# Softmax attention with a gated MLP on one Trainium2 core: next x loaded a block sooner, gate weights behind it, strips kept in order, the exponential table asked for in block one, projected sums put into rows of x

## The chip, the cores and the metric

The kernel runs on one core of one Trainium2 chip. The metric is the device time of one execution in microseconds (us); before the change the median of three runs is 2617.08 us (2616.3 to 2622.25).

## What is computed

All tensors are float32. S is 2048 rows, D is 576, F is 4608; there are 32 heads of 18 features.

```python
xn = layernorm(x)                                   # [S, D]
q, k, v = split(xn @ wqkv)                          # 32 heads x 18
o = softmax(q @ k.T * 18 ** -0.5) @ v               # per head, [S, S] scores
s = o @ wo
gate, up = xn @ W_gate, xn @ W_up                   # [S, F]
g = silu((gate * (gate > 0) * up) @ W_down)
out = x + s * g
```

Products are taken in float32 precision by splitting each operand into a rounded high part and a low remainder and adding three matmuls (high by high, high by low, low by high).

## The kernel before

**Stages.** The first 200 us normalize x, transpose it in nine chunks of 64 features per group of 512 rows, split it in high and low parts, project q, k and v, and write x, q, k and v back to HBM as `xTd`, `qd`, `kd`, `vd`. The rest is a line of 144 *blocks* `k`, made by `emit_unit` (L897). Block k works on group g of 512 rows (4 groups) and on f, one of 36 slices of 128 MLP features, so g changes at k = 36, 72 and 108; in these notes "boundary 1" is the step from block 35 to block 36, and so on. A block's first half (`up`, L696) multiplies nine chunks of x by gate and up weights (tiles `pg`, 54 matmuls on two halves of the array at once). Attention is woven into it: score matmuls for row maxima (`pm`, from `max_steps`, L244) of head pair u + 1 and score matmuls for the exponentials (`psx`, from `exp_steps`, L855) of head pair u. Sixteen blocks come before the first pair; then each of the 16 pairs u takes eight blocks. An odd block ends with 64 matmuls of attention times v (`po`, `attend`), an even one with 48 of the down projection (`py`, `down`). So two blocks are `pg`…, `po`, `pg`…, `py`.

**x.** `load_x` (L297) brings a chunk of x back from `xTd` in two DMAs (512 KB together) into pool `xA`, which has eleven buffers for the nine chunks of a group. In the last block of a group, `up` asks for the first two chunks of the next group ahead of its matmuls, and for chunk c + 2 after the last matmul that reads chunk c (L707, L717).

**Weights.** `load_up(k)` (L283) brings gate and up weights of block k (two DMAs, 576 KB together, tile `rg`, one buffer; `p` for blocks 3 to 15), `split_up` (L292) splits them on GpSimd (tile `gw`), a block ahead. `emit_unit` asks for block k + 2 at its start. `load_down` and `split_down` do the same for the down weights (`rd`, `dw`, 288 KB).

**Strips.** `strips` (L217) fetches q or k of one head pair in six small DMAs into a ring: `load_q` (tiles `kq`, `qT`) and `load_k` (`kA`, `kq`).

**Order.** Matmuls and most VectorE and GpSimd work are kept in program order. DMAs are issued by SyncE (queue SP). Its class `Maybe` keeps program order while `sp.kept` is true; from block 10 on it is false, and a scheduler may put an SP DMA anywhere its operands allow, also far ahead of where the program asks for it; `load_x` alone is always pinned. A DMA that waits on SP holds up all behind it.

**The end.** In the last head pair's block 6 four row tiles of the output are projected (`project`, L985: s in PSUM times the gate tile `gt`, then plus the row tile `xt`, then stored) with two sets of buffers; `rows_of` (L1005) loads the gate rows from `gd` and the rows of x for tile j + 2 into the buffers of tile j. In the profile these tiles are all called `gx`.

Of the kernel before, what the change touches and what calls it, by code (L numbers as in the profile page):

```python
# [9 lines left out]
F32 = mybir.dt.float32  # L10
F32R = mybir.dt.float32r
AF = mybir.ActivationFunctionType
# [7 lines left out]
def kernel(  # L20
# [11 lines left out]
    P = 128  # L32
# [77 lines left out]
    ident = consts.tile([P, P], F32, name="ident")  # L110
    make_identity(nc, ident)
    mark = consts.tile([P, 1], F32, name="mark")
    qd = dram.tile([2, D, S], F32, name="qd")
    kd = dram.tile([2, D, S], F32, name="kd")
    vd = dram.tile([NU, P, NT, HW], F32, name="vd")
# [11 lines left out]
        nc.scalar.activation(dhi, ps, AF.Copy)  # L127
        nc.vector.tensor_tensor(dlo, ps, dhi.bitcast(F32), ALU.subtract)

    def split_pool(hi, lo, raw):  # L130
        gp.tensor_copy(hi, raw)
        gp.tensor_tensor(lo, raw, hi.bitcast(F32), ALU.subtract)

    PRODUCTS = ((0, 0), (0, 1), (1, 0))

# [79 lines left out]
    tasks = []  # L215

    def strips(dst, src, u, cs, order):  # L217
        for h in range(2):
            f0 = (2 * u + h) * DH
            for b, i in enumerate(order):  # L220
                r0 = h * R + b * DH
                sp.dma_start(dst[r0 : r0 + DH].bitcast(F32), src[i, f0 : f0 + DH, cs])

    def kchunk(u, c):
        return ring[(NQ * u + c) % NRING]
# [82 lines left out]
    with ExitStack() as st:  # L308
# [2 lines left out]
        xB = pool(xBs, "xB", XC, "right")  # L311
        hx = pool(xBs, "hx", 4, "right")

        def weights(name, n, parts, pl=one, held=None, **kw):

            sl = WS if len(parts[0]) == 2 else XC
            gw = homes_w[name] if name in homes_w else pl.tile([P, 2, WS, n], F32R, name=name, **kw)
            gw = gw[:, :, :sl]
            o = 0
            for cols in parts:  # L320
                m = sum(c[2] for c in cols[0])
                rg = one.tile([P, WS, P], F32, name="rgw", bufs=2)[:, :sl, :m]
                load_nat(rg, cols)
                hi, lo = gw[:, 0, :, o : o + m], gw[:, 1, :, o : o + m]

                if held is not None:
                    held += [hi, lo, rg]
                else:
                    split_pool(hi, lo, rg)
                o += m  # L330
            return gw

# [233 lines left out]
        def qk_weights(b, **kw):  # L566
            wqk.append(
                weights(f"wqk{b}", P, [[[(wqkv, b * P, P)], [(wqkv, D + b * P, P)]]], **kw)
            )
# [4 lines left out]
        for _ in range(57):  # L574
            tp(warm[:, :P], ident, ident)
        first_rows(rows0, *held)
        qk_weights(1)
        nxt = load_rows(1)
        wvs = []

# [18 lines left out]
        for g in range(NQ):  # L599
# [46 lines left out]
            if last:  # L646
                mx = [max_steps(0, h) for h in range(2)]
                both = zip(*mx)
                deal[:] = [both, (P1 + P2) // 3, 0]
                homes = [  # L650
                    lambda: [bank("pv") for _ in range(2)],
                    lambda: [shared("pv") for _ in range(2)],
                    lambda: [psO.tile([P, 512], F32, tag="po", name="pv"), shared("pv")],
                    lambda: [bank("pv") for _ in range(2)],
                ]
                for j in range(4):
                    v_job(wv, g, j, homes[j]())
                    if j == 0:
                        split_up(1)
                    if j == 2:  # L660
                        load_up(2)
                deal[0] = None
                flush()
                for c in range(KC + 2 - XC, KC):
                    load_x(0, c)
            else:
                for j in range(4):
                    v_job(wv, g, j)
                    if j == 0 and g == 0:
                        nxt = load_rows(g + 2)  # L670
                    if j == 1:
                        spill(g, marks[-1] if g == 0 else None)
                    if j and g == NQ - 2:
                        for c in range(2 * j - 2, 2 * j):
                            load_x(0, c)
                if fill is not None:
                    for _ in fill:
                        pass
# [17 lines left out]
    def up(k):  # L696

        g, f = units[k]
        gw = gus.pop(k)
        if k < N1 and (k % 2 == 0 or k == N1 - 1):  # L700
            ps = [psO.tile([P, 512], F32, name="po"), shared("pg2")]
        else:
            ps = [bank("pg0"), bank("pg1")]
        last = f == NF - 1 and k + 1 < len(units)
        if last:
            for c in range(2):
                load_x(units[k + 1][0], c)  # L707
        xg = xcur[g]

        def ops(t, c, i, j, rows):  # L710
            return gw[rows, i, c, :], xg[c][rows, j, :]

        def half(t):
            for n, _ in enumerate(row_half(ps[t], ops, t)):
                c = n // len(PRODUCTS)
                if t and last and n % len(PRODUCTS) == 2 and c + 2 < KC:
                    load_x(units[k + 1][0], c + 2)  # L717
                yield

        return ps, [half(t) for t in range(2)]  # L720
# [72 lines left out]
    def run_tasks(todo):  # L793
        while todo:
            fn, args = todo.pop(0)
            fn(*args)
# [100 lines left out]
    def emit_unit(k, ex, ns, mx, nm):  # L897
# [5 lines left out]
        if k not in rds and k not in dws:  # L903
            load_down(k)
        split_up(k + 1)
        if k:
            load_up(k + 2)
        if k == 10:
            sp.kept = False
# [26 lines left out]
        if k == 0:  # L936
            split_up(2)
        up_end(k, ps)
        run_tasks(tasks)
        if k % 2:  # L940
            run_tasks(outs)
# [40 lines left out]
        vec(nc.vector.tensor_tensor(o5[DT:P], raw5[DT:P], o5[DT:P].bitcast(F32), ALU.subtract))  # L982
        return hf, o5

    def project(k, hf, o5, gt, xt, last=False):  # L985

        for m in range(2):
            cs = slice(m * HC, (m + 1) * HC)
            ps = shared("pw")[:, :HC]
            prs = []  # L990
            for c in range(4):
                w = wos[c]
                prs += [(hf[:, 0, c], w[:, 0, cs]), (hf[:, 0, c], w[:, 1, cs]), (hf[:, 1, c], w[:, 0, cs])]
            prs += [(o5, wos[4][:, i, cs]) for i in range(2)]
            for i, (l, w) in enumerate(prs):
                mm(ps, l, w, start=(i == 0), stop=(i == len(prs) - 1))
            vec(nc.vector.tensor_tensor(gt[:, cs], ps, gt[:, cs], ALU.mult))  # L997
            if last:
                vec(nc.vector.tensor_tensor(gt[:, cs], gt[:, cs], xt[:, cs], ALU.add))
                sp.dma_start(out2[k * P : (k + 1) * P, cs], gt[:, cs])  # L1000
        if not last:
            gp.tensor_tensor(gt, gt, xt, ALU.add)
            sp.dma_start(out2[k * P : (k + 1) * P, :], gt)

    def rows_of(k, gt, xt):  # L1005
        if k not in kept:
            sp.dma_start(gt, gd[k * P : (k + 1) * P, :])
        sp.dma_start(xt, x2[k * P : (k + 1) * P, :])

    inputs = {}  # L1010

# [15 lines left out]
    for u in range(NU):  # L1027
# [8 lines left out]
        for i in range(PER):  # L1036
# [3 lines left out]
            if not more:  # L1040
# [10 lines left out]
                if i == 6:  # L1051
# [6 lines left out]
                    split_down(k)  # L1058
                    load_down(k + 1)
                    for j in range(4):  # L1060
                        project(j, *inputs.pop(j))
                        rows_of(j + 2, sy[j % 2], sx[j % 2])
                        inputs[j + 2] = *split_heads(j + 2, spare[j % 2]), sy[j % 2], sx[j % 2]
                        if j < 2:
                            load_heads(j + 4)
                        if j == 1:
                            split_down(k + 1)
            k += 1
# [47 lines left out]
```

## Time and profile before

The profiled execution took 2619.22 us; its span, from first to last instruction, is 2617.5 us.

| | us | what it is |
|---|---|---|
| median of three runs | 2617.08 | the metric |
| profiled execution | 2619.22 | one run, its own time |
| its span | 2617.5 | the scale of all times below |
| PE busy | 2595.6 | TensorE matmuls, 99% of the span |
| DVE, ACT, POOL busy | 1907.2, 1385.3, 1204.6 | VectorE, ScalarE, GpSimd |
| PE waiting for x from HBM | 11.5 | 14 waits of at most 1.7 |

PE is the matmul engine, PEld its weight load. A row of the timeline gives start, length, engine, line, operation, out<-in by tile names, and in brackets the idle time before it and what ended it. A PE row's length is modelled, so a matmul that was held up can look busy: where time is lost is better read from how far the starts of successive pieces lie apart.

### The profile page before, as it was taken

Reading aid. Unit: us, or ns where it says so; the run is one execution under the profiler, and the core shown is the slowest. Engines: PE = TensorE matmul, PEld = TensorE weight load, DVE = VectorE, ACT = ScalarE, POOL = GpSimd, SP = SyncE. Lnnn points to the kernel's source line nnn. Section 1 sums busy time; section 2 is a strip of 40 time slices with the busy share of each in tenths; the row PEclk is TensorE's granted clock in tenths of the full one; section 3 lists DMA queues with packets and bytes.
Section 4 is the critical chain, followed back from the end, with each engine's and each line's share of the span. In section 5 each row is a group of like instructions: output and inputs, shape, how many; then the busy total and the mean of one; then the engine's idle time right before and its main releaser. Section 6 shows DMA issues by size and latency. Waiting matters only on the chain.

```text
span 2617.5 us, 54137 instructions
## 1 busy us (share of the span) xinstructions
PE 2595.6 (99%) x21845; PEld 2039.3 (78%) x21845; DVE 1907.2 (73%) x3141; ACT 1385.3 (53%) x2594; POOL 1204.6 (46%) x971
## 2 busy tenths in 40 slices
PE   9999999999999999999999999999999999999999
PEld 8898887877677777777767777787767777777788
DVE  5336677888778888888877888888877888888145
ACT  3221136655565556655556555666556655556552
POOL 4246764444364444444444444444435444444554
PEclk9999999999999999999999999999999999999999
DMA  8866422223542223222363322332254232222345
GB/s 253 274 210 159 101 55 74 66 65 75 126 104 67 71 68 80 60 72 63 76 148 85 71 71 67 75 71 71 65 126 104 70 74 66 72 58 58 71 136 190
DMA packets 263802, 253.08 MB, mean 97 GB/s; under 512 B 27648, under 2 KB 208896, under 8 KB 263552
## 3 DMA queue, kind: packets, MB, share of 16 engines
q1 hardware_dynamic: 255808, 222.48, 34.3%
q0 software_dynamic: 7744, 27.14, 3.0%
q8 instruction: 172, 2.82, 0.5%
q14 instruction: 78, 0.64, 0.1%
HBM read 203.01 MB, written 46.01 MB: 95 GB/s over the span
## 4 chain that ended last, share of the span: by engine, by line
PE 93%; DMA 3%; POOL 1%; DVE 1%; issue 1%; SPq 1%; ACT 0%; POOLq 0%; ACTq 0%; DVEq 0%
PE pg L68 31%; PE py L68 18%; PE po L68 17%; PE pm L68 11%; PE psx L68 9%; PE pq L68 3%; DMA x<-xTd 2%; PE pv L68 2%; PE pw L68 2%; POOL gw L85 0%; POOL dw L85 0%; SPq L301 0%; PE tps L76 0%; SPq L97 0%; DMA qd<-hh 0%
## 5 line engine op out<-in xcount | busy, mean ns | idle before, releaser
L270 DVE TENSOR_REDUCE mx<-pm 128x1 f32<-128x512 f32 x2048 | 1364.8, 690 | 374.0 <-PE pm L68 215.7
L68 PE MATMUL pg<-x,gw 64*128 64x512 f32 x7533 | 1376.2, 394 | 11.5 <-DMA x<-xTd 11.5
L97 ACT ACTIVATE p<-psx 128x512 f32<-128x512 f32 x2048 | 1099.6, 603 | 494.1 <-PE psx L68 444.5
L68 PEld LDWEIGHTS pg<-x,gw 64*128 64x128 f32 x7533 | 1028.9, 187 | 109.1 <-DMA x<-xTd 18.6
L85 POOL TENSOR_TENSOR hh<-h,hh 128x512 fp32r<-128x512 f32 x144 | 185.4, 1288 | 1014.3 <-ACT hh L97 970.7
L68 PEld LDWEIGHTS py<-dw,hh 128*128 128x128 f32 x3456 | 461.2, 189 | 25.9 <-DVE mx L270 18.0
L68 PE MATMUL py<-dw,hh 128*128 128x288 f32 x3456 | 478.0, 297 | 0.0
L68 PE MATMUL po<-p,va 128*32 128x512 f32 x4096 | 452.7, 594 | 0.0
L85 POOL TENSOR_TENSOR gw<-rg,gw 128x1152 fp32r<-128x1152 f32 x131 | 350.1, 2672 | 10.5
L68 PEld LDWEIGHTS po<-p,va 128*32 128x32 f32 x4096 | 126.6, 110 | 291.4 <-issue 280.7
L757 DVE TENSOR_TENSOR y<-py,y 128x288 f32<-128x288 f32 x544 | 237.0, 453 | 113.5 <-PE py L68 113.3
L68 PE MATMUL psx<-qT,kq 56*128 56x512 f32 x608 | 230.7, 393 | 0.0
L68 PE MATMUL pm<-kq,qT 54*128 54x512 f32 x608 | 228.5, 399 | 0.4 <-DVE mx L270 0.4
L85 POOL TENSOR_TENSOR dw<-rd,dw 128x576 fp32r<-128x576 f32 x144 | 206.4, 1433 | 11.5
L97 ACT ACTIVATE hh<-h 128x512 fp32r<-128x512 f32 x144 | 90.9, 631 | 214.1 <-DVE h L728 214.1
L68 PE MATMUL psx<-kq,kA 56*128 56x512 f32 x512 | 196.0, 394 | 0.2 <-DVE h L728 0.2
L68 PE MATMUL pm<-kq 54*128 54x512 f32 x512 | 195.4, 402 | 0.0
L68 PE MATMUL pm<-kA,kq 54*128 54x512 f32 x512 | 193.8, 399 | 0.9 <-DVE mx L270 0.9
L68 PE MATMUL psx<-kq 56*128 56x512 f32 x512 | 194.6, 392 | 0.0
L85 POOL CAST dw<-rd 128x576 fp32r<-128x576 f32 x144 | 95.9, 666 | 167.7 <-PE py L68 157.0
L68 PE MATMUL pm<-kA,qT 54*128 54x512 f32 x416 | 160.2, 403 | 0.0
L68 PE MATMUL psx<-qT,kA 56*128 56x512 f32 x416 | 158.4, 395 | 1.4 <-DVE gx L997 1.4
(96 smaller groups left out, 2274.1 us busy)
## 6 DMA issues: line engine op xcount, KB each, us to landing
rd<-in_B_W_down_dram SPq DMA_DIRECT2D x144, 288.0 KB
rg<-in_B_W_gate_dram SPq DMA_DIRECT2D x131, 288.0 KB
rg<-in_B_W_up_dram SPq DMA_DIRECT2D x131, 288.0 KB
x<-xTd SPq DMA_DIRECT2D x72, 256.0 KB
qd<-hh POOLq DMA_DIRECT2D x16, 512.0 KB, 4.2
kd<-hh POOLq DMA_DIRECT2D x16, 512.0 KB, 5.6
xTd<-x SPq DMA_DIRECT2D x16, 512.0 KB
kq<-kd SPq DMA_DIRECT2D x210, 36.0 KB
```

The source lines that it names most:

```text
L68: return tc.keep_in_program_order(nc.tensor.matmul(*args, **kw))
L85: return lambda *args, **kw: tc.keep_in_program_order(op(*args, **kw))
L97: i = op(*args, **kw)
L270: vec(nc.vector.tensor_reduce(mx[:, h, b, j, c : c + 1], ps, axis=AX.X, op=ALU.max))
L757: vec(nc.vector.tensor_tensor(ys[j][:, cs], ps, ys[j][:, cs], ALU.add))
```

## The change

Five edits, none of which alters a number that is computed.

1. **x and gate weights.** The first two chunks of the next group are asked for at the start of the last block but one (f = 34, `units[k + 2]`). In the last block `load_up(k + 2)` moves from the block's start to behind the request for chunk 4. Before block 0, `load_up(2)` moves behind the requests for x.
2. **Strips** of head pairs 0, 1 and 2 are pinned in program order.
3. **Exponential table.** A one-column Exp at the end of block 0.
4. **First weights.** The low part of the second q/k weight tile is made in four pieces instead of one, in the order 2, 2, 3, 2 of its nine slots.
5. **End.** The sum goes into the rows of x; the gate rows of tile j + 2 are asked for right after the sum, ahead of the store, and the rows of x after the next heads.

```diff
-    def split_pool(hi, lo, raw):
+    def split_pool(hi, lo, raw, pieces=(slice(None),)):
         gp.tensor_copy(hi, raw)
-        gp.tensor_tensor(lo, raw, hi.bitcast(F32), ALU.subtract)
+        for s_ in pieces:
+            gp.tensor_tensor(lo[:, s_], raw[:, s_], hi[:, s_].bitcast(F32), ALU.subtract)
...
     def strips(dst, src, u, cs, order):
+        queue = Kept(nc.sync) if u < 3 else sp
...
-                sp.dma_start(dst[r0 : r0 + DH].bitcast(F32), src[i, f0 : f0 + DH, cs])
+                queue.dma_start(dst[r0 : r0 + DH].bitcast(F32), src[i, f0 : f0 + DH, cs])
...
-        qk_weights(1)
+        qk_weights(1, pieces=(slice(0, 2), slice(XC, XC + 2), slice(2, XC), slice(XC + 2, WS)))
...
-                    if j == 2:
-                        load_up(2)
                 deal[0] = None
                 flush()
                 for c in range(KC + 2 - XC, KC):
                     load_x(0, c)
+                load_up(2)
...
         last = f == NF - 1 and k + 1 < len(units)
-        if last:
+        if f == NF - 2 and k + 2 < len(units):
             for c in range(2):
-                load_x(units[k + 1][0], c)
+                load_x(units[k + 2][0], c)
...
                     load_x(units[k + 1][0], c + 2)
+                    if c == 2:
+                        load_up(k + 2)
...
-        if k:
+        if k and (units[k][1] < NF - 1 or k + 1 == len(units)):
             load_up(k + 2)
...
         up_end(k, ps)
+        if k == 0:
+            pinned(nc.scalar.activation(first_exp, ident[:, :1], AF.Exp))
...
-            gp.tensor_tensor(gt, gt, xt, ALU.add)
-            sp.dma_start(out2[k * P : (k + 1) * P, :], gt)
+            gp.tensor_tensor(xt, gt, xt, ALU.add)
+            if refill:
+                refill()
+            sp.dma_start(out2[k * P : (k + 1) * P, :], xt)
...
-                        project(j, *inputs.pop(j))
-                        rows_of(j + 2, sy[j % 2], sx[j % 2])
+                        project(j, *inputs.pop(j), refill=lambda: gate_of(j + 2, sy[j % 2]))
                         inputs[j + 2] = *split_heads(j + 2, spare[j % 2]), sy[j % 2], sx[j % 2]
                         if j < 2:
                             load_heads(j + 4)
+                        x_of(j + 2, sx[j % 2])
```

`gate_of` and `x_of` are the two halves of `rows_of`. The order of instructions on PE and DVE is the same as before; ACT's has the table load moved and one activation more, POOL's three pieces more; SP's changes most. The rows below are SP's queue.

SP around boundary 1, before: x<-xTd are the loads of x (18 DMAs, nine chunks), rd the down weights of blocks 35 and 36, rg the gate and up weights of blocks 37 and 38, od<-on attention results stored in block 34.

```order
L97 DMA od<-on 18x512 x2
L97 DMA rd<-in_B_W_down_dram 128x576
L97 DMA rg<-in_B_W_gate_dram 64x9x128
L97 DMA rg<-in_B_W_up_dram 64x9x128
L301 DMA x<-xTd 64x1024 x18
L97 DMA rd<-in_B_W_down_dram 128x576
```

The same place now:

```order
L97 DMA od<-on 18x512 x2
L304 DMA x<-xTd 64x1024 x4
L97 DMA rd<-in_B_W_down_dram 128x576
L304 DMA x<-xTd 64x1024 x6
L97 DMA rg<-in_B_W_gate_dram 64x9x128
L97 DMA rg<-in_B_W_up_dram 64x9x128
L304 DMA x<-xTd 64x1024 x8
L97 DMA rd<-in_B_W_down_dram 128x576
```

Two chunks moved past the down weights into block 34, three more past the gate weights of block 37, and those stand ahead of the last four. Boundaries 2 and 3 read alike.

SP ahead of block 0, before: qT<-qd are q strips of head pair 1, kA<-kd k strips of pair 2, rg the weights of block 2, rd those of block 0.

```order
L97 DMA kq<-kd 18x512 x6
L97 DMA qT<-qd 18x1024 x12
L97 DMA rg<-in_B_W_gate_dram 64x9x128
L97 DMA rg<-in_B_W_up_dram 64x9x128
L97 DMA kA<-kd 18x512 x6
L301 DMA x<-xTd 64x1024 x6
L97 DMA rd<-in_B_W_down_dram 128x576
```

The same place now:

```order
L85 DMA kq<-kd 18x512 x6
L304 DMA x<-xTd 64x1024 x6
L97 DMA rg<-in_B_W_gate_dram 64x9x128
L97 DMA rg<-in_B_W_up_dram 64x9x128
L97 DMA rd<-in_B_W_down_dram 128x576
```

Eighteen strips left this place for that of the program's request (around blocks 13 to 16), and x stands ahead of the weights of block 2.

SP in the projections, before: gx<-gd are gate rows, gx<-in_A_x_dram rows of x, out_dram<-gx stores, ro and r heads.

```order
L97 DMA out_dram<-gx 128x576
L97 DMA gx<-in_A_x_dram 128x576
L97 DMA ro<-od 128x4x128
L97 DMA r_32981<-od 64x128
L97 DMA gx<-gd 128x576
L97 DMA out_dram<-gx 128x576
```

The same place now:

```order
L97 DMA gx<-gd 128x576
L97 DMA out_dram<-gx 128x576
L97 DMA ro<-od 128x4x128
L97 DMA r_32986<-od 64x128 x2
L97 DMA gx<-in_A_x_dram 128x576
L97 DMA gx<-gd 128x576
```

The gate rows moved ahead of the store, the rows of x behind the heads.

More of the change, by code (lines that the diff above doesn't have):

```diff
@@ L112 @@
     mark = consts.tile([P, 1], F32, name="mark")
+    first_exp = consts.tile([P, 1], F32, name="first_exp")
     qd = dram.tile([2, D, S], F32, name="qd")
@@ L312, with weights @@
         hx = pool(xBs, "hx", 4, "right")
-        def weights(name, n, parts, pl=one, held=None, **kw):
+        def weights(name, n, parts, pl=one, held=None, pieces=(slice(None),), **kw):
             sl = WS if len(parts[0]) == 2 else XC
@@ L328, in weights @@
                 else:
-                    split_pool(hi, lo, rg)
+                    split_pool(hi, lo, rg, pieces)
                 o += m
@@ L983, in split_heads, with project @@
         return hf, o5
-    def project(k, hf, o5, gt, xt, last=False):
+    def project(k, hf, o5, gt, xt, last=False, refill=None):
         for m in range(2):
@@ L1001, in project, with gate_of, x_of, rows_of @@
         if not last:
-            gp.tensor_tensor(gt, gt, xt, ALU.add)
-            sp.dma_start(out2[k * P : (k + 1) * P, :], gt)
-    def rows_of(k, gt, xt):
+            gp.tensor_tensor(xt, gt, xt, ALU.add)
+            if refill:
+                refill()
+            sp.dma_start(out2[k * P : (k + 1) * P, :], xt)
+    def gate_of(k, gt):
         if k not in kept:
             sp.dma_start(gt, gd[k * P : (k + 1) * P, :])
+    def x_of(k, xt):
         sp.dma_start(xt, x2[k * P : (k + 1) * P, :])
+    def rows_of(k, gt, xt):
+        gate_of(k, gt)
+        x_of(k, xt)
     inputs = {}
```

## The prediction

> **What bounds the kernel now.** I read the page first: the busy time by engine and the shares of the chain that ended last.
>
> ```profile
> PE 2595.6 (99%) x21845; PEld 2039.3 (78%) x21845; DVE 1907.2 (73%) x3141; ACT 1385.3 (53%) x2594; POOL 1204.6 (46%) x971
> ...
> PE 93%; DMA 3%; POOL 1%; DVE 1%; issue 1%; SPq 1%; ACT 0%; POOLq 0%; ACTq 0%; DVEq 0%
> ```
>
> TensorE sets the time. No edit removes a matmul, so the only thing to gain is time in which PE is held up, and 99% busy says little about it, since a matmul that is held up counts as busy. So I went to the chain in order of time, where every block pair shows its `po` piece, and looked for pairs that are too long.
>
> ```profile
> 626.29 7.00 PE po L68 x64
> ...
> 660.31 7.00 PE po L68 x64
> 677.54 6.16 PE py L68 x45
> ...
> 736.44 7.00 PE po L68 x64
> ...
> 1281.65 7.00 PE po L68 x64
> ...
> 1354.89 7.00 PE po L68 x64
> ...
> 1899.86 7.00 PE po L68 x64
> ...
> 1974.74 7.00 PE po L68 x64
> ```
>
> A pair of blocks takes 660.31 - 626.29 = 34.02 us. The two pairs that hold boundary 1 take 736.44 - 660.31 = 76.13 where 68.04 is due: **8.1 us lost**. Boundary 2: 1354.89 - 1281.65 = 73.24, **5.2 lost**. Boundary 3: 1974.74 - 1899.86 = 74.88, **6.8 lost**. Together 20.1 us, three places in 2617. What happens there is in the table of 4 us windows (stretch, its length, busy time of PE, PEld, DVE, ACT and POOL, granted clock, DMA share, GB/s) and, for boundary 1, in the timelines of SP and of PE.
>
> ```profile
> 700.00:704.00 4.00, 4.00 (x36) 2.50 (x30) 2.18 (x4) 2.50 (x5) 3.35 (x5) 1.00 1.03 255
> ...
> 712.00:716.00 4.00, 2.41 (x14) 1.44 (x16) 1.48 (x3) 1.69 (x3) 0.00 (x0) 0.81 1.14 234
> 716.00:720.00 4.00, 4.00 (x18) 3.16 (x15) 2.85 (x5) 1.03 (x2) 0.00 (x0) 0.50 0.16 31
> ```
>
> ```profile
> 669.79 0.90 SPq L97 DMA_DIRECT2D od<-on  x2
> 685.96 0.36 SPq L97 DMA_DIRECT2D rd<-in_B_W_down_dram  x1
> 689.83 0.60 SPq L97 DMA_DIRECT2D rg<-in_B_W_gate_dram  x1
> ...
> 692.02 14.99 SPq L301 DMA_DIRECT2D x<-xTd  x18
> ```
>
> ```profile
> 713.57 0.50 PE L68 MATMUL pg<-x,gw 64*128 64x512 f32 x1 [1.68 <-DMA x<-xTd]
> ```
>
> The first load of x is issued at 692.02, behind gate weights that wait for their buffer until 689.83, though block 35 began at about 684.1 (the `py` piece at 677.54 plus 6.5). From then the DMA engines are full (share 1.03, 255 GB/s), and PE waits for chunk after chunk until 713.57. Then the granted clock falls to 0.50 for some 4 us.
>
> **Boundaries.** The move takes the wait's cause away. Nine chunks came in 713.57 - 692.02 = 21.55 us, 2.4 us each. Now two of them are asked for behind the od stores (669.79, block 34), sixteen us before the rush. At 685.96, behind the down weights, chunk 2 follows as soon as PE has left chunk 0; then 3, 4, the gate weights, 5 to 8. By sizes in the code the down and gate weights are 0.55 and 1.1 chunks, so 7 + 0.55 + 1.1 = 8.65 chunks at 2.4 us end at 686.4 + 20.8 = 707.2. PE begins block 36 at about 701.3 and reads nine chunks in a block's 10.2 us (677.54 - 667.3, the `po` end at 660.31 + 7.0), so it needs chunk 8 at 701.3 + 9.0 = 710.3, and chunk 5, which lands near 700, at 707. Margin 3 us or more for each. So the waits should go entirely: **20.1 us**, bounds 15 (what a residue of a little under 2 us a boundary leaves) and 20.1. What is late next: the gate weights of block 37, issued at about 690 as now but landing some 6 us later, near 697; GpSimd splits them from 701, so that is hidden by half of block 35. The chunks moved into block 34 pass nothing that PE waits for there.
>
> The fallen clock is part of those 20.1 us: boundary 2 lost 5.2 with the clock at full rate, boundaries 1 and 3 lost 2.9 and 1.6 more.
>
> ```profile
> 1332.00:1336.00 4.00, 2.64 (x18) 1.58 (x18) 2.04 (x4) 2.17 (x4) 0.00 (x0) 1.00 1.07 251
> ...
> 1952.00:1956.00 4.00, 2.46 (x14) 1.77 (x14) 1.29 (x3) 1.19 (x2) 0.00 (x0) 0.69 1.10 213
> ```
>
> I take it to go with the waits, since it comes right behind the longest of them. The Trainium skill (TensorE: Matmul & The Clock Gate, section "What's actually happening") says that the array falls to half rate after at least one idle window of about 3.4 us; here it fell after waits of at most 1.68 us each, so either the windows count something softer than idleness or the fall is not the waits' own. By the rule read strictly the 4.5 us stay (a rival below).
>
> **Block 0.** The same in small, by the timelines of SP and PE.
>
> ```profile
> 195.75 5.47 SPq L301 DMA_DIRECT2D x<-xTd  x6
> ```
>
> ```profile
> 204.91 0.39 PE L68 MATMUL po<-x,gw 64*128 64x512 f32 x1
> ...
> 205.13 0.39 PE L68 MATMUL po<-x,gw 64*128 64x512 f32 x1
> ...
> 207.07 0.50 PE L68 MATMUL pg<-x,gw 64*128 64x512 f32 x1 [1.49 <-DMA x<-xTd]
> ```
>
> Starts lie 0.22 us apart, then 1.94: 1.7 us lost. The loads wait for buffers that PE leaves only at about 195, so they cannot start much sooner; but the strips and weights in front of them are gone. I take half, **0.9 us**, bounds 0 and 1.8. The weights of block 2, now behind x, land near 207, when GpSimd comes to split them; if they are late, block 2 waits for at most the 1 to 2 us they moved.
>
> **Strips.** Of the strips that the scheduler had pulled forward, twelve ran just when stores of q were due (SP, ACT, PE timelines):
>
> ```profile
> 179.00 7.59 SPq L97 DMA_DIRECT2D qT<-qd  x12
> ```
>
> ```profile
> 184.80 0.60 ACT L127 ACTIVATE hh<-pq 128x512 fp32r<-128x512 f32 x1 [1.49 <-DMA qd<-hh]
> ```
>
> ```profile
> 186.77 0.50 PE L68 MATMUL pm<-kA,kq 54*128 54x512 f32 x1 [0.95 <-DVE mx L270]
> ```
>
> ACT waits 1.49 us for a store to leave its buffer, VectorE stands behind it, PE 0.95 us behind that. Without the strips: **0.9 us**, bounds 0 and 1.2. At their new places, between blocks 13 and 24, they are hidden by blocks of 17 us; if not, six of them cost the 3.8 us that half of the row at 179.00 shows.
>
> **Table.** The load of the exponential's table, ACT's idle time behind block 0, and PE's starts around the load:
>
> ```profile
> 360.32 1.28 ACT L97 ACT_TABLE_LOAD   x1
> ```
>
> ```profile
> 215.03 0.60 ACT L97 ACTIVATE h<-pg 128x512 f32<-128x512 f32 x1 [4.77 <-PE pg L68]
> ```
>
> ```profile
> 360.42 0.50 PE L68 MATMUL psx<-kq,kA 56*128 56x512 f32 x1
> 361.08 0.50 PE L68 MATMUL psx<-kq,kA 56*128 56x512 f32 x1 [0.16 <-DVE h L728]
> ...
> 362.02 0.49 PE L68 MATMUL pm<-kq,qT 54*128 54x512 f32 x1 [0.44 <-DVE mx L270]
> ```
>
> Gaps of 0.66 and 0.94 where 0.22 is usual: **1.2 us**, nearly the load's length. Behind block 0 ACT is idle for 4.77 us, so the load costs nothing there; bounds 0.9 and 1.3. The Trainium skill (ScalarE: Activation LUTs, "What ACT_TABLE_LOAD costs") puts a switch at 2.66 us with a drain, which would make this term 2.6 and the sum 1.4 larger; the row shows 1.28.
>
> **First weights.** GpSimd's low part (POOL) and PE behind it:
>
> ```profile
> 15.28 2.67 POOL L85 TENSOR_TENSOR wqk<-rgw,wqk 128x1152 fp32r<-128x1152 f32 x1
> ```
>
> ```profile
> 18.01 16.26 PE L68 MATMUL pq<-x,wqk 64*128 64x512 f32 x140 [0.50 <-POOL wqk L85]
> ```
>
> The first two pieces, 4/9 of 2.67 us, end at about 16.6, before PE comes at 17.5: **0.8 us** with the slowed matmul ahead of the gap, bounds 0.3 and 1.0. Three more starts on GpSimd cost it about 0.2 us, where nobody waits.
>
> **End.** The chain and PE's row:
>
> ```profile
> 2538.36 1.81 POOL gx L85
> 2540.17 0.02 issue
> 2540.19 3.19 DMA out_dram<-gx
> ...
> 2543.43 4.59 DMA gx<-gd
> ```
>
> ```profile
> 2548.65 0.86 PE L68 MATMUL psx<-qT,kA 56*128 56x512 f32 x2 [1.36 <-DVE gx L997]
> ```
>
> PE waits for a PSUM bank that VectorE empties only when gate rows have come, and these wait for a store to leave their buffer. Now they start at the sum's end, 2540.2, and come 3.2 us sooner, which is more than PE's wait: **1.6 us** with the slowed restart, bounds 0 and 1.8. Late next are the rows of x of tiles 2 and 3, behind heads and, for tile 3, behind gate rows of tile 4 on SP. GpSimd's sums wait for them, and behind those on GpSimd the remainder `hh` of the last block; PE has that block's `pg` and 7 us of `po` to cover it.
>
> **Sum.** 20.1 + 0.9 + 0.9 + 1.2 + 0.8 + 1.6 = 25.5 us. PE runs without a break between these places and to the last projection, so I let all of it reach the end. The profiled execution took 2619.22 us by its own time: 2593.7. It lies 2.1 over the median of the runs, 2617.08, so the median should come to **2591.6 us**. All lower bounds give 15 + 0 + 0 + 0.9 + 0.3 + 0 = 16.2, so 2600.9; all upper ones 27.2, so 2589.9.
>
> **Rivals.**
>
> *The clock falls all the same.* If the half-rate stretch at boundaries 1 and 3 comes from the clock's own windows and not from the waits, 4.5 us stay: 2596.1. For it: it follows waits of 1.7 us only, and boundary 2, with waits in all of its last chunks, has none. Against: it comes right behind the longest waits. Chance 0.08. (This is what the strict reading of the page on the clock gate, cited above, gives.)
>
> *x is still late.* If the DMA engines, with stores and strips beside them, bring a chunk only every 3.0 us, chunk 8 lands at 686.4 + 26 = 712.4, 2 us after its need; at 3.6 us a chunk it is 7 us. Of the gain 6 to 15 us would go, and the time would be 2598 to 2607. For it: the share is already over 1 there, and GpSimd's stores use the same engines. Against: the 2.4 us were measured under just that load. Chance 0.08 for more than 2600.
>
> *The wait moves to the gate weights.* PE is through with x, but the weights of block 37, now behind three chunks, reach GpSimd late, and block 37 waits in place of block 36. Block 37 starts at 718 if nothing waits (701.3 + 10.2 + 6.5), and a split takes GpSimd about 4 us, so to eat 6 us a boundary they would have to land near 720, over 20 us later than I reckon. Then the gain is some 7 us: 2610, no change that can be told. Chance 0.04.
>
> *Slower: strips block the queue.* In program order a strip waits on SP until PE has left its ring buffer, and the down and gate weights behind it wait too. Eight groups of strips (of pairs 1 and 2) are concerned. Weights are asked for two blocks ahead and split one ahead, so a wait under one block (17.0 us, half of 34.02) costs nothing, and what exceeds it costs PE in full. If each group stood 21 us, 8 x 4 = 32 us are lost: 2591.6 + 32 = 2623.6. Against: the order on SP puts each group next to weights of the block in which its buffer comes free. Chance 0.03.
>
> That the change does not do what it says I rule out: the order on SP shows x ahead, and PE's and VectorE's orders are unaltered.
>
> **The numbers.** The forecast has 0.77, the fallen clock 0.08, late x 0.08, weights 0.04, strips 0.03. The range 2588 to 2600 holds the first two (0.85, a little less for their tails): its ends are the sums of the bounds, with a microsecond or two for the runs' scatter below. A difference of 0.3%, 7.9 us, is about what a measurement of this kernel can tell from no change. Faster by more needs under 2609.2: forecast, clock and late x, 0.93. Within: 0.04. Slower: 0.03.
>
> **What would show it.** In the new profile the `po` pieces around each boundary lie 68 us apart, no PE row around block 36 has a wait for x, and the granted clock stays at 1.00 there; the table load stands near 209; PE's gaps near 185, 206, 360 and 2547 are gone. I am wrong if PE waits for x or for `gw` in blocks 36 to 38, or if a pair of blocks between 16 and 40 takes more than 34.1 us.

## The result and the profile after

| | before | after |
|---|---|---|
| median of 6 runs (lowest, highest) | 2618.61 us (2616.30, 2622.25) | 2601.21 us (2600.33, 2602.55) |
| profiled execution, its own time | 2619.22 us | 2600.33 us |
| its span | 2617.5 us | 2598.6 us |

The ratio is 0.9933, with a 95% interval of 0.992 to 0.9946: faster, by 17.4 us. The forecast was 2591.6 us, range 2588 to 2600. So the direction came, and a third of the gain did not.

The page of the kernel after, busy time by engine and the chain's shares by engine:

```profile
PE 2589.2 (100%) x21845; PEld 2017.2 (78%) x21845; DVE 1912.9 (74%) x3141; ACT 1382.1 (53%) x2595; POOL 1204.4 (46%) x974
...
PE 98%; DVE 1%; DMA 1%; POOL 0%; issue 0%; SPq 0%; ACT 0%; POOLq 0%; ACTq 0%
```

DMA's share of the chain fell from 3% to 1%. The chain in order of time shows the boundaries, each row a `po` piece (start, length):

```profile
662.01 7.00 PE po L68 x64
...
696.03 7.00 PE po L68 x64
...
730.30 7.00 PE po L68 x64
...
1275.38 7.00 PE po L68 x64
...
1343.70 7.00 PE po L68 x64
...
1888.87 7.00 PE po L68 x64
...
1957.17 7.00 PE po L68 x64
```

The two pairs at a boundary now take 68.29, 68.32 and 68.30 us, where 76.13, 73.24 and 74.88 stood. TensorE's order is the same in both kernels, so the start of one and the same matmul can be held against itself. At boundary 1 the `po` piece goes from 1.70 us late (662.01 against 660.31) to 6.14 early (730.30 against 736.44): 7.84 us won. Boundary 2: 6.27 to 11.19 early, 4.92 won. Boundary 3: 10.99 to 17.57, 6.58. Together 19.3 of the 20.1 forecast. No wait of PE for x or `gw` is left between 684 and 724 us, and the 4 us windows that had a clock of 0.81, 0.50 and 0.69 are at full rate (columns as before: PE, PEld, DVE, ACT, POOL, clock, DMA share, GB/s):

```profile
712.00:716.00 4.00, 4.00 (x33) 3.55 (x30) 3.96 (x9) 1.90 (x4) 0.00 (x0) 1.00 0.17 46
716.00:720.00 4.00, 4.00 (x31) 3.84 (x31) 2.40 (x7) 0.00 (x0) 1.80 (x2) 1.00 0.49 139
...
1952.00:1956.00 4.00, 4.00 (x37) 3.37 (x36) 3.29 (x7) 3.85 (x8) 3.83 (x5) 1.00 0.53 123
```

But look at the first of those `po` rows: at 662 us the changed kernel is 1.7 us **behind**, where the terms of the opening (0.8, 0.9, 0.9, 1.2) should have put it 3.8 ahead. 5.5 us are missing, all of them ahead of 370 us. Held against itself at many places, the same matmul tells where:

| stretch (us) | what happens | forecast | won (+) or lost (-) |
|---|---|---|---|
| to 18 | first weights | +0.8 | +0.7 |
| 20 to 35, 104 to 132 | `pq` matmuls run slower | 0 | -0.8 |
| 184 to 189 | strips | +0.9 | +0.8 |
| 203 to 209 | x of block 0 | +0.9 | +0.6 |
| 217 to 224 | block 2 waits | 0 | -2.4 |
| 228 to 359 | blocks 2 to 15 run slower | 0 | -1.0 |
| 359 to 370 | table | +1.2 | +0.5 |
| 684 to 1960 | boundaries | +20.1 | +19.3 |
| 2530 to 2612 | end | +1.6 | +1.4 |

The nine rows add to 19.1 us; the span lost 18.9. Three of the rows were forecast at nothing. One is **block 2**. The timelines of SP and of POOL, kernel after:

```profile
195.08 5.77 SPq L304 DMA_DIRECT2D x<-xTd  x6
200.95 0.63 SPq L97 DMA_DIRECT2D rg<-in_B_W_gate_dram  x1
201.62 0.90 SPq L97 DMA_DIRECT2D rg<-in_B_W_up_dram  x1
```

```profile
210.07 1.15 POOL L85 CAST gw<-rg 128x1152 fp32r<-128x1152 f32 x1 [6.40 <-DMA rg<-in_B_W_up_dram]
211.31 2.67 POOL L85 TENSOR_TENSOR gw<-rg,gw 128x1152 fp32r<-128x1152 f32 x1
213.93 1.29 POOL L85 TENSOR_TENSOR hh<-h,hh 128x512 fp32r<-128x512 f32 x1
...
220.42 0.66 POOL L85 CAST dw<-rd 128x576 fp32r<-128x576 f32 x1 [3.06 <-DMA rd<-in_B_W_down_dram]
```

The same two casts in the kernel before:

```profile
208.11 1.15 POOL L85 CAST gw<-rg 128x1152 fp32r<-128x1152 f32 x1 [3.77 <-PE po L68]
...
218.46 0.67 POOL L85 CAST dw<-rd 128x576 fp32r<-128x576 f32 x1 [3.08 <-DMA rd<-in_B_W_down_dram]
```

Before, GpSimd came to the weights when PE had left their buffer; now it stands 6.40 us for their transfer, which the chain shows as one piece of 8.31 us from its issue:

```profile
201.62 8.31 DMA rg<-in_B_W_up_dram
```

What stood in its way is not x alone: GpSimd issued four stores of v (288 KB each) at 193.45 and 199.82, and from 194 to 211 us the engines moved 3.65 MB. GpSimd's work is kept in program order, so the remainder `hh`, the down weights and the request for the next ones (`rd`, in the buffer that GpSimd has to empty) all move by 2 us, and the `py` of block 2 waits twice on PE's timeline:

```profile
222.62 0.40 PE L68 MATMUL py<-dw,hh 128*128 128x288 f32 x1 [0.96 <-POOL dw L85]
223.85 2.40 PE L68 MATMUL py<-dw,hh 128*128 128x288 f32 x16 [0.82 <-POOL hh L85]
```

The other two are a **slower TensorE**, with no wait at all. The timeline of PE has a run of a hundred `pq` matmuls near 110 us, before and after:

```profile
109.95 11.55 PE L68 MATMUL pq<-x,wqk 64*128 64x512 f32 x100
```

```profile
109.58 11.84 PE L68 MATMUL pq<-x,wqk 64*128 64x512 f32 x100
```

And in the chain, from one `py` to the fourth behind it (eight blocks), before 82.63 us (263.33 to 345.96), after 83.25:

```profile
263.33 6.55 PE py L68 x48
...
345.96 6.55 PE py L68 x48
```

```profile
264.93 6.59 PE py L68 x48
...
348.18 6.59 PE py L68 x48
```

The granted clock is 1.00 in all of it. Behind 370 us nothing more is lost to it: from 378 to 660 us the changed kernel takes 281.7 us and the kernel before 281.8. So the theories: (a) block 2's weights behind x cost 2.4 us; (b) something slows TensorE in these stretches, and the candidates are the strips at their new places, the table loaded early, the way PE restarts after a wait, and, after the first four experiments, the places of the tiles in memory.

### The profile page after: what moved, and what is told of

It reads as the page before. It is cut to its first block, busy times and chain, and to the rows that moved or that the text cites. A ratio compares the mean times of both kernels' runs of the same rounds, so it can differ in the third digit from the quotient of the medians.

```text
span 2598.6 us, 54145 instructions
## 1 busy us (share of the span) xinstructions
PE 2589.2 (100%) x21845; PEld 2017.2 (78%) x21845; DVE 1912.9 (74%) x3141; ACT 1382.1 (53%) x2595; POOL 1204.4 (46%) x974
## 4 chain that ended last, share of the span: by engine, by line
PE 98%; DVE 1%; DMA 1%; POOL 0%; issue 0%; SPq 0%; ACT 0%; POOLq 0%; ACTq 0%
PE pg L68 31%; PE po L68 19%; PE py L68 18%; PE pm L68 11%; PE psx L68 10%; PE pq L68 4%; PE pw L68 2%; PE pv L68 2%; PE tps L76 0%; DMA rg<-in_B_W_up_dram 0%; DMA xt<-in_A_x_dram 0%; POOL dw L85 0%; DMA rd<-in_B_W_down_dram 0%; POOL hh L85 0%; DVE hh L129 0%
## 5 line engine op out<-in xcount | busy, mean ns | idle before, releaser
L68 PE MATMUL pg<-x,gw 64*128 64x512 f32 x7533 | 1362.2, 393 | 0.9 <-DMA x<-xTd 0.9
L68 PEld LDWEIGHTS pg<-x,gw 64*128 64x128 f32 x7533 | 1016.9, 186 | 97.2 <-issue 4.0
L85 POOL CAST gw<-rg 128x1152 fp32r<-128x1152 f32 x131 | 157.3, 1201 | 12.1 <-DMA rg<-in_B_W_up_dram 12.1
```

The lines of the kernel that those rows point to most:

```text
L68: return tc.keep_in_program_order(nc.tensor.matmul(*args, **kw))
L85: return lambda *args, **kw: tc.keep_in_program_order(op(*args, **kw))
```

## The experiments

All times below are medians of 4 to 11 runs, beside medians of the kernel before of 2619.0 to 2619.9 us on the same chips; the profile of each gives the stretches. Those medians of one and the same kernel lie 0.9 us apart, so smaller differences between experiments say little. "x100" is the row near 110 us, "eight blocks" the stretch of the `py` rows.

**Weights of block 2 ahead of x.**

```diff
                     if j == 0:
                         split_up(1)
+                    if j == 2:
+                        load_up(2)
...
-                load_up(2)
```

> The changed kernel with one step undone: the gate weights of block 2 are asked for ahead of x again (all else stays, strips in order too). Theory (the missing 5.5 us of the opening are mostly block 2's weights, which stood behind x and landed at 209.9): the DMA engines are idle from 190 to 194 us, so these weights land before x starts at about 195; x keeps its start; GpSimd's cast of block 2's weights waits for PE, not for a transfer, and begins near 207.5; the 2.4 us lost in block 2 come back. If the slower rate of TensorE in blocks 2 to 15 (1.0 us) came from the way block 2 restarts after its wait, that comes back too. Time: 2601.2 - 2.4 = 2598.8 with the slow rate kept, 2597.8 without. Rival (the order of SP is not the cause: strips or the engines' load make block 2 late): 2601 as now. Rival (weights ahead of x delay x as before): 2601.2 - 2.4 + 0.6 = 2599.4.

2599.89 us, ratio 0.9921 (0.9909 to 0.9934), span 2596.2, 2.4 under the changed kernel's. POOL's timeline:

```profile
206.58 1.15 POOL L85 CAST gw<-rg 128x1152 fp32r<-128x1152 f32 x1 [2.90 <-PE po L68]
```

PE releases it again, block 2 loses 0.1 us in place of 2.4, and x is issued at 195.09 as before the repair (195.08): SP had waited for x's buffers, and in the changed kernel the engines were idle from 190 to 194 us. So (a) is shown. Whether the move of these weights bought x anything is not: block 0's x gains 0.9 here, but over all kernels with strips in order PE waits 0.1 to 1.8 us for it with the weights ahead (nine profiles, mean 1.0) and 0.2 to 0.9 with the weights behind (seven, mean 0.7). The slow rate stays (83.25), so a restart after block 2's wait is not its cause.

**Boundary edit alone, on the kernel before.**

```diff
-        if last:
+        if f == NF - 2 and k + 2 < len(units):
             for c in range(2):
-                load_x(units[k + 1][0], c)
+                load_x(units[k + 2][0], c)
...
+                    if c == 2:
+                        load_up(k + 2)
...
-        if k:
+        if k and (units[k][1] < NF - 1 or k + 1 == len(units)):
```

> The kernel before with the boundary edit alone (x two chunks a block sooner, gate weights behind the fifth chunk). Theory (the boundaries gave 19.2 us of the 20.1 that were forecast, and the other edits together give nothing): profiled time 2619.2 - 19.2 = 2600.0, median of the runs 2618.6 - 19.2 = 2599.4, so a little faster than the changed kernel. Rival (the boundaries need the other edits, or these give their forecast 5.4 us): 2606 or more.

2599.11 us, ratio 0.9921 (0.9908 to 0.9933), span 2596.7: one edit gives as much as all five. Its rate is the fast one (x100 11.55, eight blocks 82.62). Two of its rows matter below: with the strips still pulled forward PE has no wait near 186, and ACT waits half as long for the store as in the profile of before (1.49).

```profile
177.17 8.09 SPq L97 DMA_DIRECT2D qT<-qd  x12
```

```profile
183.63 0.60 ACT L127 ACTIVATE hh<-pq 128x512 fp32r<-128x512 f32 x1 [0.70 <-DMA qd<-hh]
```

**First weights in one piece.**

```diff
-        qk_weights(1, pieces=(slice(0, 2), slice(XC, XC + 2), slice(2, XC), slice(XC + 2, WS)))
+        qk_weights(1)
```

> The changed kernel with GpSimd's low part of the first weights in one piece, as before. Theory (the 0.8 us won at 18 us are given back, because TensorE runs its pairs of half-array matmuls at 0.233 us in place of 0.227 until some later wait): PE waits 0.5 us near 17.5 again, then 28 matmuls of pq take 3.18 us, not 3.26, and by 180 us PE stands within 0.2 us of where the changed kernel stands. Time 2601.2, no change. Rival (the 0.8 us are kept and something else loses them): PE is 0.8 us later at 180 us and the time is 2602.0. Rival (the rate has nothing to do with the wait): 28 matmuls take 3.26 us with the wait too, and the time is 2602.0.

2602.81 us, span 0.9 over the changed kernel's, and x100 11.84: the last rival. My theory, that the missing wait brings the slow rate, falls: the wait of 0.41 us is there and the rate is slow.

**No early exponential.**

```diff
         if k == 0:
-            pinned(nc.scalar.activation(first_exp, ident[:, :1], AF.Exp))
+            pass
```

> The changed kernel without the early exponential, so that the table is loaded at the first exponential again. Theory (the early load gains 0.65 us near 360 and costs nothing): TensorE loses 0.65 us near 360 against the changed kernel; the slower rate in blocks 2 to 15 stays; 2601.2 + 0.65 = 2601.9. Rival (the table switched early slows ScalarE's Relu and Copy in blocks 1 to 15, which is the loss of 1.0 us there): the loss between 228 and 359 us goes, and the time is 2600.9.

2603.78 us; eight blocks 83.28: the early table doesn't slow anything. Near 360 us the changed kernel gains 0.55 on this one: that is what the early load is worth. (This profile starts 1 us later and loses another 1 us ahead of block 2, so its total says less than its stretches.) What was left in this kernel and in the three slow ones, and not in the fast ones, was the four-byte tile `first_exp`, which I had not counted as an edit. It is the last tile of its pool, and in the compiled program every tile on that side of the memory starts 32 bytes later: x from 19104 to 19136, `gw` from 68768 to 68800. The other side (k, q, p, the down weights and the x of the first and third row group in the projections) stays.

**Exponential into a word that is there.**

```diff
-    first_exp = consts.tile([P, 1], F32, name="first_exp")
...
-            pinned(nc.scalar.activation(first_exp, ident[:, :1], AF.Exp))
+            pinned(nc.scalar.activation(mark, ident[:, :1], AF.Exp))
```

> The changed kernel, with the early exponential written into the word `mark` that is there already, so that no new tile `first_exp` is made. The new word takes 32 bytes at the head of every partition and moves every tile on that side (x, the gate and projection weights, hh) from an address that is 32 over a multiple of 64 bytes to a multiple of 64. Theory (TensorE's slower rate at 20 to 35, at 104 to 132 and at 228 to 359 us is this shift: it is there in the three kernels that hold the word and gone in the one that has the boundary edit alone): the rate is again that of the kernel before, 28 matmuls of pq near 20 us take 3.18 us, the 1.0 us between 228 and 359 and the 0.4 and 0.5 us before that come back, block 2 still loses its 2.4 us: 2601.2 - 1.9 = 2599.3. Rival (the strips at their new places slow TensorE): nothing changes, 2601.2.

2599.51 us, where the theory has 2599.3; eight blocks 82.63, and x100:

```profile
109.60 11.55 PE L68 MATMUL pq<-x,wqk 64*128 64x512 f32 x100
```

**The word alone, on the kernel before.**

```diff
     mark = consts.tile([P, 1], F32, name="mark")
+    spare_word = consts.tile([P, 1], F32, name="spare_word")
+    nc.gpsimd.memset(spare_word, 0.0)
```

> The kernel before with a word of four bytes more among the constants, which nothing reads, and nothing else. Theory (the shift of the addresses by 32 bytes alone slows TensorE): 28 matmuls of pq near 20 us take 3.26 us in place of 3.18, the stretch from 228 to 359 us is 1.0 us longer, PE is 1.9 us later at 360 us: 2618.6 + 1.9 = 2620.5, within the scatter of the runs, so read from the trace. Rival (strips, or the order of SP, are the cause): no stretch changes, 2618.6.

2621.96 us, ratio 1.0009 (1.0001 to 1.0018), and the slow rate, in the timeline of PE and in the chain:

```profile
110.08 11.84 PE L68 MATMUL pq<-x,wqk 64*128 64x512 f32 x100
```

```profile
263.73 6.59 PE py L68 x48
...
346.98 6.59 PE py L68 x48
```

83.25 us, as in the changed kernel. With the four-byte tile the slow rate comes, without it (the run before) it goes, and neither strips nor table come into it: (b) is the places of the tiles.

**Both repairs.** The edits of the first and of the fifth experiment together.

> The changed kernel with both repairs: the gate weights of block 2 ahead of x, and the exponential into `mark`. Theory (the losses are separate and add): 2601.2 - 2.4 - 1.9 = 2596.9, of it profiled 2598.6 - 4.3 = 2594.3 of span. Rival (the slow rate is not the address): 2599 as with the weights alone.

2596.52 us (2595.77 to 2597.44), ratio 0.9909 (0.9896 to 0.9923): the losses add, and every run is under the lowest of the changed kernel (2600.33).

**Two words more** (the changed kernel with the spare word besides).

> The changed kernel with one more unused word, so that all tiles on that side move by another 32 bytes and stand 32 over a multiple of 64 again, 64 bytes from where they were before. Theory (what counts is the address within 64 bytes): the fast rate comes back, as with no new word, 2599.3. Rival (the shift counts by itself, or by 128 bytes or more, or the new tile costs in some other way): the rate stays slow, 2601.2.

2601.98 us; the rate is neither theory's but lies between: x100 11.77, eight blocks 82.80. Block 2 lost 4.1 us here: after its two waits of 1.1 and 0.8 us the clock fell to 0.57 for 4 us, in the windows:

```profile
220.00:224.00 4.00, 2.29 (x14) 1.37 (x10) 1.15 (x2) 0.00 (x0) 3.14 (x3) 1.00 0.93 211
224.00:228.00 4.00, 3.80 (x17) 3.81 (x18) 0.69 (x1) 2.28 (x5) 3.92 (x4) 0.57 0.98 202
```

**All but the boundary edit.** The changed kernel with the second diff taken back.

> The changed kernel without the boundary edit (x and gate weights at a boundary as before), all other edits in. Theory (the boundaries bring 19.2 us, the other edits nothing, since what strips, table, first weights and end gain goes into the weights of block 2 and into the slower rate): PE some 1.7 us later than the kernel before from block 16 to the end, then 1.9 us won at the end: 2619 +- 1.5, no change. Rival (the other edits give 4 us or more, and the boundaries less in this company): 2615 or less.

2624.07 us, ratio 1.0017 (1.0008 to 1.0026). Slower than expected: block 2 costs 3.7 us in this execution (behind its two waits the clock fell to 0.58 in the window from 224 to 228), so that PE is 3.6 behind at 355 us, and the boundaries, with their waits, lose 4.6 us more than in the profile of before, where the clock fell at two of them and here at all three. Boundary 2 alone accounts for 3.6 of these: its clock stood at 0.77, 0.50 and 0.88 in the windows from 1338 to 1350, half speed for 6.8 us in all, which costs up to 3.4. Whether the other edits made it fall there or chance did is open. Only the end gives 2.0 back. The other edits, as made, cost more than they bring.

**Both repairs, strips free again.**

```diff
-        queue = Kept(nc.sync) if u < 3 else sp
+        queue = sp
```

> The kernel with both repairs (exponential into `mark`, weights of block 2 ahead of x), with the scheduler free again to pull strips forward. Theory (the 0.95 us that PE waited near 187 belonged to that one execution: with the same strips two other executions show waits of 0 and 0.3 us): between nothing and 0.8 us lost, 2596.5 to 2597.3. Rival (the strips cost what was forecast): 2597.4 and a PE gap of about 1 us near 186 in this profile too. Rival (strips ahead of x delay x): PE's wait for x in block 0 grows from under 0.6 us to 1.5.

2597.24 us, span 1.4 over that of both repairs. The table of waits of PE, 178 to 216 us:

```profile
PE pg L68 <- DMA x<-xTd: 1.6, 1, 1.6
PE pm L68 <- DVE mx L272: 0.5, 1, 0.5
```

In the profile of both repairs x costs one wait of 0.1 us, and the second row is not there. The wait near 186 was 0.95 us in the profile of before, 0 with the boundary edit alone, 0.3 with the word alone, 0.5 here: the theory of one execution holds. The wait for x in block 0 grew as the last rival has it, but one pair of profiles shows less than it seems to: eight other profiles with strips in order and weights ahead show 0.3 to 1.8 us there, the four with strips free 1.4 to 1.6. So strips ahead of x may cost it half a microsecond on average (means 1.5 and 1.0), which these scatters do not settle, and the runs overlap (2597.04 to 2597.64 against 2595.77 to 2597.44).

**Both repairs, old end.**

```diff
-            gp.tensor_tensor(xt, gt, xt, ALU.add)
-            if refill:
-                refill()
-            sp.dma_start(out2[k * P : (k + 1) * P, :], xt)
+            gp.tensor_tensor(gt, gt, xt, ALU.add)
+            sp.dma_start(out2[k * P : (k + 1) * P, :], gt)
...
-                        project(j, *inputs.pop(j), refill=lambda: gate_of(j + 2, sy[j % 2]))
+                        project(j, *inputs.pop(j))
+                        rows_of(j + 2, sy[j % 2], sx[j % 2])
...
-                        x_of(j + 2, sx[j % 2])
```

> The kernel with both repairs, with the old end (sums into gate rows, gate rows and rows of x asked for together behind the sum's store). Theory (the end edit brings what the trace shows, 1.7 us by the last projection): 2596.5 + 1.7 = 2598.2, and PE's wait of 1.3 us for the bank near 2525 is there again. Rival (the end's gain is lost again in the last projections): 2596.5.

2598.70 us, 2.2 over both repairs; 1.8 of it arises behind 2530 us in the profiles, and the wait is back:

```profile
PE psx L68 <- DVE gx L1003: 1.4, 1, 1.4
```

**Which places are slow?** Seven placements: the changed kernel with a word at the edge of the other side too, and the kernel with both repairs with unused words on the left side (x, weights), on the right (k, q, p) or on both.

```diff
     right = ctx.enter_context(ExitStack())
+    spare_word = pool(right, "edge", 1, "right").tile([P, 1], F32, name="spare_word")
+    nc.gpsimd.memset(spare_word, 0.0)
```

> The changed kernel with a word of four bytes at the edge of the other side of the memory too, so that the tiles of both sides stand at multiples of 64 bytes (in the kernel before all stand 32 over one, in the changed kernel x, the weights and hh at multiples, and k, q and p 32 over). Theory (slow are two streams that run beside each other with addresses that differ by 32 within 64 bytes): the fast rate comes back, 28 matmuls of pq near 20 us in 3.18 us, PE 1.0 us sooner through 228 to 359 us, 2601.2 - 1.9 = 2599.3. Rival (32 over a multiple of 64 is the fast place, a multiple the slow one): k, q and p are slow now too; pq stays at 3.26 us, and the stretches from 360 us on become slower as well, by as much as 1 per cent: 2602 to 2620.

> The kernel with both repairs (median 2596.5) with an unused word of four bytes on the left side: x, weights and hh move by 32 bytes to multiples of 64, k, q and p stay 32 over. As in the kernel before with the word. Theory of unlike places (two streams beside each other whose addresses differ by 32 within 64 bytes run slower) and theory of the left place (x and weights at multiples of 64 are slow): pq at 3.26 us for 28 near 27 us, not 3.18; 0.4 us lost from 104 to 132 us, 1.0 us from 228 to 355. Theory of chance (the rate is set by how the streams start after a wait, not by the place): any of it may be missing.

> The same kernel with two unused words on the left side: all tiles are 32 over a multiple of 64 again, x and weights 64 bytes further on. Unlike places, and left place: the fast rate, nothing lost from 104 to 132 us and from 228 to 355. Theory of chance: any. If it loses about 0.25 us from 228 to 355, as the changed kernel with two words did, the distance counts beyond 64 bytes.

> The same kernel with an unused word at the edge of the right side alone: k, q, p and the x of the first and third group of rows move to multiples of 64, the weights and the other x stay 32 over. Unlike places: slow again, 0.4 us lost from 104 to 132 us and 1.0 us from 228 to 355. Left place: the fast rate everywhere. Chance: any.

> The same kernel with both words, so that all tiles stand at multiples of 64. Unlike places: the fast rate everywhere, as with no word. Left place: slow, 0.4 us lost from 104 to 132 us and 1.0 us from 228 to 355. Chance, or a rule of more than one term: between the two.

> The repaired kernel with three unused words on the left side: its tiles stand 96 bytes further from those of the right side than in the kernel before. In the runs so far the time of one fixed stretch (four block pairs, from a py to the fourth py behind it, 264 to 346 us) was 82.63 us wherever both sides kept their old distance, 83.25 with 32 bytes more, 82.80 with 64 more, whichever side moved. Theory (the distance counts, with a period of 128 bytes): 96 is 32 the other way and as slow, 83.25 or near. Rival (a period of 64): 83.25 and for 64 more 82.63, which the runs already speak against. Rival (any other distance than the old one is slow, more or less by chance): anything above 82.63.

> The same with four unused words, 128 bytes. Theory (period of 128 bytes): the fast rate, 82.63 us for the stretch and 11.55 us for the hundred pq near 110 us, and the repaired kernel's time, 2596.5. Rival (longer period, or no period): 82.8 or more, and 2598.

Tiles on the right are laid out from the far end, so a word there moves them the other way. What both sides have moved against each other orders all kernels, the four earlier ones too:

| moved apart by | kernels | x100 | eight blocks |
|---|---|---|---|
| 0 | before; boundary edit alone; `mark`; both repairs, also with old strips or old end | 11.55 | 82.62 to 82.63 |
| 32 | after and its variants with the new word; word alone; left word (2599.19); right word (2598.83) | 11.84 | 83.25 to 83.28 |
| 64 | two words; word on both sides (2600.93); left two words (2598.20); left and right (2598.33) | 11.77 | 82.80 |
| 96 | left three words (2597.27) | 11.85 | 83.07 |
| 128 | left four words (2595.74) | 11.79 | 82.20 |

Each of my theories falls. A place of its own within 64 bytes is not it: one word on the left and one on the right are equally slow. A period of 64 or of 128 is not it either: in the eight blocks 64 and 96 lie between 0 and 32 (`pq` at 96 is as slow as at 32), and 128 bytes makes the projections slow and the blocks faster than they ever were, 82.20, with a total as good as that of both repairs. Shown is that the distance between the tiles of the two sides sets TensorE's rate in these two stretches, within 2.6% for `pq` and 1.3% for the blocks, the same in every kernel with that distance (96 and 128 have one kernel each). It fits that `pq` slows only where x lies on the right and its weights on the left (20 to 35 and 104 to 132 us): from 37 to 104, most of it with both on the left, 32 bytes cost about 0.1 us. And it is not everywhere: from 378 to 660 us all twenty kernels take 281.6 to 282.0 us, in no order of distance. Which two reads meet, and by what rule, stays open.

## Why the prediction was right and where it failed

- **Boundaries: right.** The waits went, 19.3 of 20.1 us, and the edit alone gives them. The two pairs at a boundary still take 0.26 us over 68.04, with no wait on PE, and the pair behind them takes 34.58 (730.30 to 764.88). By its own sign ("a pair of blocks between 16 and 40 takes more than 34.1 us") the prediction would be wrong here, but the sign was badly chosen: before the change that next pair took 34.52 too (736.44 to 770.96), so 34.02 is not due at every place.
- **The clock: right.** It fell to 0.50 at two or three of the three boundaries in each of the three profiles that have the waits (before, the word alone, all but the boundary edit), and at none in the seventeen others, so it goes with the waits. (At boundary 1 it was down for longer than "some 4 us": 0.81, 0.50 and 0.84 in the windows from 712 to 724 make 6.8.) The Trainium skill (TensorE: Matmul & The Clock Gate, "What's actually happening") has a window that runs freely, so that a wait may or may not be caught: that fits, since seven kernels had nearly the same two waits in block 2 (0.8 to 1.1 us, then 0.8) and only two of them lost the clock there (two words more, all but the boundary edit). That it takes an idle window of 3.4 us does not fit: no single wait there was over 1.1 us.
- **Weights of block 2: the failed step.** "The weights of block 2, now behind x, land near 207, when GpSimd comes to split them", and so were costed at nothing; the "1 to 2 us" that block 2 would wait "if they are late" went into neither the sum nor the bounds. They were asked for at 200.95 and 201.62 and landed at 209.93. I took no account of what stood in front of the transfer, which took 8.31 us behind x's 1.5 MB and beside 1.15 MB of v stores, and I stopped at the cast instead of following it through GpSimd to the request for the down weights. Cost: 2.4 us.
- **"PE runs without a break between these places and to the last projection, so I let all of it reach the end": failed too.** Besides the waits for x of block 0 and in block 2 there was no break, but PE ran slower: 1.8 us by a tile of four bytes that I took for part of the table edit and gave no price.
- **Table: oversized.** 0.55 us for 1.2. PE's two gaps went, but the matmuls behind them took some of it back.
- **Strips: right by luck.** The 0.95 us was that one execution's; the three others with strips free show 0 to 0.5, so against them the 0.8 in the table is the draw of that profile. That strips in order let x come sooner is not shown beyond its scatter.
- **First weights, x of block 0, end:** 0.7 of 0.8 at 18 us, 0.6 of 0.9, 1.4 of 1.6. That the first reaches the end is not shown: against the profile of before, from 15 to 37 us, the sixteen kernels with the pieces win -0.3 to 0.7, the three others without them 0.1 to 0.4. (The four pieces took GpSimd 3.11 us in place of 2.67, 0.4 more and not 0.2.) The second is -0.3 to 0.9 in the nine kernels with block 2 mended and strips in order.
- **From the profile to the median: 3.0 us.** I took the profiled execution of before as 2.1 over the median of three runs; against six runs it is 0.6 over (2619.22, 2618.61), and that of after, the fastest of its six runs, is 0.9 under its median. Which execution is profiled is chance, and no bound held it.

The opening missed by 5.5, the boundaries by 0.8, the end by 0.2 and the median by 3.0: 9.5 of the 9.6 us between 2591.6 and 2601.21.

## What to carry to other kernels

When a request is moved behind another, price the landing and not the issue (all bytes that move in that time, other queues' stores too, at the rate that a row shows), and follow each engine that stands in order behind the one that waits, down to the next request it makes. Count a new tile as an edit, however small: hold the same matmul against itself in both traces, and where it drifts without a wait, look at what moved in memory. A wait seen in one execution that hangs on DMA timing is worth a range from nothing, and so is one that is missing in one execution; the waits that came back at every boundary of every execution were the ones to bank on.

## What the hardware showed that I had not expected

- Moving x and the weights by 32, 64, 96 or 128 bytes against k, q and p changes the time of the same matmuls at full clock: a hundred `pq` from 11.55 to 11.85 us, eight blocks from 82.20 to 83.28. The Trainium skill (SBUF — State Buffer, "SBUF: two separate sides") says that TensorE never waits on anyone for its ports; no run here tests that, but the same matmuls do not run at one rate wherever their operands lie.
- The transfer of 288 KB of up weights needed 8.31 us from its issue, behind six of 256 KB and one of 288 and beside stores, where the DMA share stood at 1.01 and 1.15 (windows from 200 to 208 us).
- Waits of 1.1 and 0.8 us, 0.4 us of work between them, brought the clock to 0.57 in a window of 4 us; of seven kernels with such a pair of waits (0.8 to 1.1 us, then 0.8) two lost the clock and five did not.
